# Sums over two taps in f32 for two quarters instead of one, in the middle chunks of an attention and GLU kernel

## The chip, the cores and the metric

The kernel runs on one core of a Trainium2 chip. A core has five engines with queues of their own: TensorE (PE; matrix products, which write to PSUM), VectorE (DVE; elementwise work), ScalarE (ACT; activation functions and copies out of PSUM), GpSimd (POOL) and SyncE (SP), which here issues all DMAs. The engines wait for each other by semaphores. The metric is the device time of one execution in microseconds; less is better.

## The reference

```python
x = A_x                                  # 1 x 2048 x 512
xn = layernorm(x)
q, k, v = split(xn @ wqkv)               # 32 heads of 16
# token s sees s, s-2, ..., s-14: 8 taps, dilation 2
logits = einsum("bhsd,bhswd->bhsw", q, k[s - 2 w]) * 16 ** -0.5
attn = softmax(where(s - 2 w >= 0, logits, -1e9))
o = einsum("bhsw,bhswd->bhsd", attn, v[s - 2 w])
s_ = o @ wo
g = silu((gelu(xn @ w_gate) * (xn @ w_up)) @ w_down)   # 1792 wide inside
return x + s_ * g
```

Matrices are bf16.

## The kernel before

The 2048 tokens go through in four chunks `j` of 512 (`TQ`). For each chunk TensorE runs three stages: `glu` (14 groups `fc` of 128 inner columns; each 4 matmuls into `g_ps` and 4 into `u_ps`), `qkv` of the next chunk (12 groups of 4 matmuls), and `down` (4 token tiles of 14 matmuls into `y_ps`), after which `finish` multiplies in the attention's result (`s_ps`). The attention is fitted in between.

The schedule is manual: each engine's order is the order of the calls. The table `side` lists, by `at(key, fn, ...)`, what is called ahead of a step; `("glu", j, fc)` means ahead of group `fc` of chunk `j`, and so ahead of that group's `h` product on VectorE.

The steps that matter:

- `glu` (L461): ScalarE makes `ge = gelu(g_ps)` and `u` from PSUM, VectorE multiplies them into `h`. `ge` and `u` have three buffers each (`sm`), and the PSUM pool `mm` has four banks.
- `qk_products` (L320): in the qkv stage of the next chunk VectorE makes the 8 products `pk` of `q` with shifted `k`, each in two halves, 16 instructions. `logits` (L339) sums them over the 16 elements of a head on TensorE (`L_ps`), and ScalarE writes `E = exp(L_ps)`. The taps lie in `E` as 4 `wl` on the partitions (32 heads each) times 2 `wh` along the free dimension.
- `load_v` (L300): four DMAs bring `v` into `v_arr`, one for each `wl`, shifted, so that 128 partitions hold 32 heads by 4 taps.
- `av_product(j, g, wh)` (L401): the product of `E` for one `wh` with 4 of the 16 elements of `v` (a quarter `g`), written as bf16 `pv`. In chunks 2 and 3 it is made in two instructions, `n = 2`.
- `av_pair(j, g, d)` (L414): one element of a quarter, both `wh` at once in f32 (`two`), then an addition of the two halves into bf16 `pv`. It does on VectorE the sum over `wh` that otherwise TensorE does.
- `av_sums` (L434): TensorE sums `pv` over the four `wl` for each quarter. A quarter made by `av_product` takes 8 matmuls (4 for each `wh`), one made by `av_pair` takes 4. Each writes 32 partitions, 128x512 moving.
- `sums` (L532), called after the first `y_ps` tile of a chunk (for the last chunk, ahead of glu group 12): denominators, `av_sums`, the next chunk's logits, then the reciprocals, and the loads of the next `v_arr`.

Before the change quarter 0 of chunks 1 to 3 is made by pairs, ahead of groups 2, 4, 6 and 8; the other three quarters by six `av_product`, ahead of 1, 3, 5, 7, 9 and 10. Chunk 0 uses `av_product` alone. The tile `two` shares a buffer with `q_sb` (tag `q` of the pool `qp`, one buffer). `pk` and `pv` rotate through the 12 buffers of the pool `prod`; from chunk 1 on the second four `pk` share a buffer with `v_arr`.

Of the kernel before, what the change touches and what calls it, by code (L numbers as in the profile page):

```python
# [8 lines left out]
ALU = mybir.AluOpType  # L9
AF = mybir.ActivationFunctionType  # L10
BF16 = mybir.dt.bfloat16
F32 = mybir.dt.float32

P = 128
# [5 lines left out]
WH = 2  # L20
PAD = 16
TQ = 512
# [6 lines left out]
def kernel(  # L29
# [13 lines left out]
    nc = tc.nc  # L43
    B, S, D = A_x.shape
    DF = B_w_gate.shape[1]
    NT, NC, NF, NJ = S // P, D // P, DF // P, S // TQ
# [6 lines left out]
    def pool(name, bufs, **kw):  # L53
        return ctx.enter_context(tc.tile_pool(name=name, bufs=bufs, **kw))
# [4 lines left out]
    qp = pool("qp", 1)  # L59
# [3 lines left out]
    prod = pool("prod", 12)  # L63
    hp = pool("hp", 14)
    xtp = pool("xtp", 2)
    op = pool("op", 1)
# [48 lines left out]
    def load_late_weights():  # L115
# [18 lines left out]
        out=vT.rearrange("(k p) n -> p k n", p=P)[:, :, 0:PAD],  # L134
# [134 lines left out]
    st = [dict(pk={}, pv={}, vst={}) for _ in range(NJ)]  # L269

    def copy_out(j, fo, ps, i0=0, n=TQ, m=1, copy=None):

        which, c = divmod(fo, NC)
        if which == 0:
            if "q" not in st[j]:
                st[j]["q"] = qp.tile([P, NC, TQ], BF16, name="q_sb", tag="q")
            dst = st[j]["q"][:, c : c + m, i0 : i0 + n]
        elif which == 1:
            dst = k_sb[j][:, c : c + m, PAD + i0 : PAD + i0 + n]
        else:  # L280
            if c // 2 not in st[j]["vst"]:
                st[j]["vst"][c // 2] = vsp.tile([P, 2, TQ], BF16, name="vst")
            dst = st[j]["vst"][c // 2][:, c % 2 : c % 2 + m, i0 : i0 + n]
        if copy is None:
            nc.scalar.activation(out=dst, in_=ps, func=AF.Copy)  # L285
        else:
            copy(out=dst, in_=ps)
        if which == 2 and (c + m) % 2 == 0 and i0 + n == TQ:
            r, lo = slice((c // 2) * 2 * P, (c // 2 + 1) * 2 * P), PAD + j * TQ
            nc.sync.dma_start(  # L290
                out=vT[r, lo : lo + TQ].rearrange("(c p) n -> p c n", p=P),
                in_=st[j]["vst"][c // 2][:],
            )

    def qkv(j, fo):
        ps = mm.tile([P, 1, TQ], F32, name="qkv_ps", tag="mm")
        project(ps[:, 0, :], wqkv_sb, fo * P, j)
        copy_out(j, fo, ps[:])
# [102 lines left out]
    def av_product(j, g, wh):  # L401
        pv = prod.tile([P, 4, TQ], BF16, name="pv", tag="prod")
        lo = WL * DIL * (1 - wh)
        n = 4 if j < 2 else 2
        for d in range(0, 4, n):
            nc.vector.tensor_tensor(  # L406
                out=pv[:, d : d + n, :],
                in0=st[j]["E"][:, wh, :].unsqueeze(1).to_broadcast([P, n, TQ]),
                in1=st[j]["va"][:, 4 * g + d : 4 * g + d + n, lo : lo + TQ],
                op=ALU.mult,  # L410
            )
        st[j]["pv"][g, wh] = pv

    def av_pair(j, g, d):  # L414

        if d == 0:
            st[j]["pv"][g] = prod.tile([P, 4, TQ], BF16, name="pv", tag="prod")

            st[j]["two"] = qp.tile([P, WH, TQ], F32, name="two", tag="q")
        two = st[j]["two"]  # L420
        v = st[j]["va"][:, 4 * g + d, 0:TQ]
        nc.vector.tensor_tensor(  # L422
            out=two[:],
            in0=st[j]["Eb"][:],
            in1=bass.AP(
                tensor=v.tensor, offset=v.offset, ap=[v.ap[0], [WL * DIL, WH], [1, TQ]]
            ),
            op=ALU.mult,
        )
        nc.vector.tensor_tensor(  # L430
            out=st[j]["pv"][g][:, d, :], in0=two[:, 0, :], in1=two[:, 1, :], op=ALU.add
        )
# [78 lines left out]
    def at(key, fn, *args):  # L511
        side.setdefault(key, []).append((fn, args))
# [16 lines left out]
    for i in range(8):  # L529
        at(("glu", 0, 9 + i) if i < 5 else ("qkv", 1, 0), av_product, 0, i // 2, i % 2)  # L530
# [15 lines left out]
    for j in range(1, NJ):  # L546
        at(("qkv", j, 2), k_halo, j)
        for i in range(2):
            at(("qkv", j, 4 + 4 * i), qk_products, j, range(W), 2 * i, 2)

        for i in range(6):
            at(("glu", j, 1 + i + min(i, 4)), av_product, j, 1 + i // 2, i % 2)
        for d in range(4):
            at(("glu", j, 2 + 2 * d), av_pair, j, 0, d)
    at(("glu", NJ - 1, 12), sums, NJ - 1)


# [4 lines left out]
    pairs = [(8 + 2 * i, mm.tile([P, 2, HQ], F32, name="v_ps", tag="mm")[:]) for i in range(2)]  # L562
# [58 lines left out]
    for fo, ps in pairs:  # L621
        copy_out(0, fo, ps, 0, HQ, 2, nc.vector.tensor_copy if fo >= 8 else None)
# [5 lines left out]
    for n, fo in enumerate((0, 2, 4, 6, 8, 10)):  # L628
        ps = mm.tile([P, 2, HQ], F32, name="qkv_ps", tag="mm")

        w = HQ if n else P
        for i0 in range(0, HQ, w):
            for i in range(2):
                project(ps[:, i, i0 : i0 + w], wqkv_sb, (fo + i) * P, 0, HQ + i0, w)
        copy_out(0, fo, ps[:], HQ, HQ, 2)
# [65 lines left out]
```

## Time and profile before

| what | value |
|---|---|
| median of 5 runs | 226.8 us (226.61 to 226.99) |
| the profiled execution | 226.97 us, of which the span is 225.3 |
| granted TensorE clock | 0.999 |
| VectorE busy | 164.3 us (73%) |
| ScalarE busy | 131.4 us (58%) |
| glu stage of chunk 1 on TensorE | 73.26 to 97.44 us |
| qkv of chunk 2 on TensorE | 97.44 to 107.80 us |
| `sums` of chunk 1 on TensorE (`den_ps`, `o_ps`, `L_ps`) | 110.82 to 114.28 us |
| glu stage of chunk 2 | 126.91 to 151.08 us |
| glu stage of chunk 3, with its sums | 180.55 to 206.56 us |
| `v_arr` loads, issue to landing | 5.3 / 8.5 / 12.6 us (least, median, most) |

Times in the views count from the first instruction of the span. A row of the groups names the line, the engine, the operation, what is written and read, partitions x elements with their types, and the count; then the busy time in us and the mean of one in ns; then the idle time of the engine just ahead of such instructions and what ended most of it. A line of the timeline gives start and length in us, and in brackets the idle time ahead of it and what released it. The page's rows L261 `g_ps` and `u_ps` (57.5 us each), L479 `y_ps` (49.9 us) and L261 `qkv_ps` (37.0 us) hold most of TensorE's time; L332 `pk` (38.9 us), L406 `pv` (32.3 us), L471 `h` (23.5 us) and L422 `two` (14.6 us) most of VectorE's.

### The profile page before, as it was taken

What the parts mean: (1) busy time and instruction counts of PE and PEld (TensorE: products, weight loads), DVE (VectorE), ACT (ScalarE), POOL (GpSimd) and SP (SyncE); (2) the same over time, 40 slices, a digit from 0 to 9 for tenths busy, and PEclk for the clock granted to TensorE, in tenths of its full rate; (3) what the DMA queues carried; (4) which work ended last, traced back from release to release, by engine and by line L of the source; (5) the groups of instructions that cost most, each with busy time, mean ns of one, the idle gap of its engine ahead of it and who ended that gap; (6) DMA issues with size and microseconds to landing.
All of it is one profiled execution on the core that took longest, in us unless ns stands there. A gap on an engine that the chain in (4) does not pass through costs nothing.

```text
span 225.3 us, 3583 instructions
## 1 busy us (share of the span) xinstructions
PE 221.3 (98%) x1322; PEld 106.6 (47%) x1322; DVE 164.3 (73%) x295; ACT 131.4 (58%) x207; POOL 21.6 (10%) x67
## 2 busy tenths in 40 slices
PE   8999999999999999999999999999999999999994
PEld 4994444444444444444444444444444444444443
DVE  5588973999984799819983799944944389992452
ACT  4476679767631767676751476767763357666211
POOL 1025981000120000000040000000000000000000
PEclk9999999999999999999999999999999999999999
DMA  6999699972079910000229950000117950001002
GB/s 196 379 401 264 135 197 150 361 218 96 11 153 200 209 23 0 0 3 1 93 52 214 187 146 3 0 0 0 67 41 156 198 138 1 0 0 30 3 23 70
DMA packets 30258, 24.89 MB, mean 111 GB/s; under 512 B 11040, under 2 KB 29728, under 8 KB 30240
## 3 DMA queue, kind: packets, MB, share of 16 engines
q1 hardware_dynamic: 30240, 24.66, 46.8%
q8 instruction: 10, 0.16, 0.3%
q14 instruction: 8, 0.07, 0.1%
HBM read 18.74 MB, written 4.34 MB: 102 GB/s over the span
## 4 chain that ended last, share of the span: by engine, by line
PE 98%; DVE 0%; ACT 0%; issue 0%
PE y_ps L479 22%; PE g_ps L261 22%; PE u_ps L261 21%; PE qkv_ps L261 16%; PE s_ps L495 6%; PE L_ps L352 3%; PE o_ps L442 3%; PE qk_ps L574 2%; PE v_ps L574 1%; PE warm_ps L244 1%; PE qk_ps L565 1%; PE den_ps L372 0%; PE v_ps L565 0%; PE trb L220 0%; PE tr L220 0%; DVE m L503 0%
## 5 line engine op out<-in xcount | busy, mean ns | idle before, releaser
L261 PE MATMUL g_ps<-xnT,wg_sb 128*128 128x512 bf16 x224 | 57.5, 379 | 0.0
L261 PE MATMUL u_ps<-xnT,wu_sb 128*128 128x512 bf16 x224 | 57.5, 379 | 0.0
L479 PE MATMUL y_ps<-wd_sb,h 128*128 128x512 bf16 (+2 forms) x238 | 49.9, 367 | 0.0
L467 ACT ACTIVATE ge<-g_ps 128x512 bf16<-128x512 f32 x56 | 33.5, 598 | 16.9 <-PE g_ps L261 16.8
L332 DVE TENSOR_TENSOR pk<-q_sb,k_sb 128x1024 bf16<-128x1024 bf16 (+1 forms) x56 | 38.9, 759 | 5.9 <-ACT k_sb L285 5.9
L469 ACT ACTIVATE u<-u_ps 128x512 bf16<-128x512 f32 x56 | 33.5, 598 | 16.6 <-PE u_ps L261 16.6
L261 PE MATMUL qkv_ps<-xnT,wqkv_sb 128*128 128x512 bf16 (+2 forms) x200 | 37.0, 345 | 0.0
L479 PEld LDWEIGHTS <-h 128*128 128x128 bf16 x238 | 22.6, 98 | 26.5 <-issue 1.3
L406 DVE TENSOR_TENSOR pv<-E,v_arr 128x1024 bf16<-128x1024 bf16 (+1 forms) x38 | 32.3, 880 | 3.7 <-DMA v_arr<-vT 3.7
L261 PEld LDWEIGHTS <-wu_sb 128*128 128x128 bf16 x224 | 21.9, 98 | 26.4
L261 PEld LDWEIGHTS <-wg_sb 128*128 128x128 bf16 x224 | 21.7, 98 | 26.6 <-issue 0.8
L471 DVE TENSOR_TENSOR h<-ge,u 128x512 bf16<-128x512 bf16 x56 | 23.5, 420 | 14.2 <-ACT u L469 13.9
L487 ACT ACTIVATE sl<-y_ps 128x512 bf16<-128x512 f32 (+2 forms) x17 | 9.7, 572 | 32.7 <-PE y_ps L479 32.7
L261 PEld LDWEIGHTS <-wqkv_sb 128*128 128x128 bf16 x200 | 18.9, 98 | 17.4
L503 DVE TENSOR_TENSOR m<-s_ps,sl 128x512 bf16<-128x512 f32 (+2 forms) x17 | 11.1, 654 | 19.8 <-PE s_ps L495 19.7
L204 POOL TENSOR_TENSOR rstd<-rstd,mhalf 128x1 f32<-128x1 f32 x12 | 7.0, 583 | 90.7 <-DVE rstd L201 90.7
L495 PE MATMUL s_ps<-wo_sb,oT 128*128 128x512 bf16 (+2 forms) x68 | 14.8, 366 | 0.0
L422 DVE TENSOR_TENSOR two<-E,v_arr 128x1024 f32<-128x1024 bf16 x12 | 14.6, 1216 | 0.0
L454 DVE TENSOR_TENSOR oT<-o_ps,rb 128x1024 bf16<-128x1024 f32 x8 | 9.4, 1218 | 6.8 <-DMA rb<-rs_d 6.5
L285 ACT ACTIVATE vst<-qkv_ps 128x512 bf16<-128x512 f32 x14 | 8.4, 598 | 3.7 <-PE qkv_ps L261 3.7
L285 ACT ACTIVATE k_sb<-qkv_ps 128x512 bf16<-128x512 f32 x14 | 8.4, 602 | 3.2 <-PE qkv_ps L261 3.2
L285 ACT ACTIVATE q_sb<-qkv_ps 128x512 bf16<-128x512 f32 x14 | 8.3, 603 | 3.0 <-PE qkv_ps L261 3.0
(65 smaller groups left out, 143.4 us busy)
## 6 DMA issues: line engine op xcount, KB each, us to landing
v_arr<-vT SPq DMA_DIRECT2D x16, 520.0 KB, 8.5
vT<-vst SPq DMA_DIRECT2D x8, 256.0 KB, 2.2
out_dram<-o_t SPq DMA_DIRECT2D x15, 128.0 KB, 2.9
wg_sb<-in_B_w_gate_dram SPq DMA_DIRECT2D x2, 896.0 KB, 10.0
wu_sb<-in_B_w_up_dram SPq DMA_DIRECT2D x2, 896.0 KB, 12.2
wd_sb<-in_B_w_down_dram SPq DMA_DIRECT2D x1, 1792.0 KB, 11.4
wqkv_sb<-in_A_wqkv_dram SPq DMA_DIRECT2D x4, 384.0 KB, 4.5
x_sb<-in_A_x_dram SPq DMA_DIRECT2D x3, 512.0 KB, 7.8
```

What stands on the lines that cost most here:

```text
L261: nc.tensor.matmul(ps, lhsT=w[:, dk, lo : lo + P], rhs=xnT[j][:, dk, i0 : i0 + n], start=(dk == 0), stop=(dk == NC - 1),)
L285: nc.scalar.activation(out=dst, in_=ps, func=AF.Copy)
L332: nc.vector.tensor_tensor(out=st[j]["pk"][w][:, c0 : c0 + n, :], in0=st[j]["q"][:, c0 : c0 + n, :], in1=k_sb[j][:, c0 : c0 + n, off : off ...
L406: nc.vector.tensor_tensor(out=pv[:, d : d + n, :], in0=st[j]["E"][:, wh, :].unsqueeze(1).to_broadcast([P, n, TQ]), in1=st[j]["va"][:, 4 * ...
L422: nc.vector.tensor_tensor(out=two[:], in0=st[j]["Eb"][:], in1=bass.AP(tensor=v.tensor, offset=v.offset, ap=[v.ap[0], [WL * DIL, WH], [1, T ...
L467: nc.scalar.activation(out=ge[:], in_=g_ps[:], func=AF.Gelu_apprx_tanh)
L469: nc.scalar.activation(out=u[:], in_=u_ps[:], func=AF.Copy)
L471: nc.vector.tensor_tensor(out=h[:], in0=ge[:], in1=u[:], op=ALU.mult)
L479: nc.tensor.matmul(y[:], lhsT=st[j][fc][:, tt * P : (tt + 1) * P], rhs=wd_sb[:, fc, cols], start=(fc == 0), stop=(fc == NF - 1),)
L487: nc.scalar.activation(out=sl[:], in_=y[:], func=AF.Silu)
L495: nc.tensor.matmul(s[:], lhsT=st[j]["oT"][:, g, tt * P : (tt + 1) * P], rhs=wo_sb[:, g, cols], start=(g == 0), stop=(g == NC - 1),)
L503: nc.vector.tensor_tensor(out=m[:], in0=s[:], in1=sl[:], op=ALU.mult)
```

## The change

In chunks 1 and 2, quarters 0 and 1 are made by pairs and quarters 2 and 3 by `av_product`; chunk 3 keeps one quarter by pairs. The calls are spread over other glu groups: in chunks 1 and 2 pairs ahead of groups 1, 2, 3, 5, 6, 8, 10 and 11 and products ahead of 0, 7, 12 and 13; in chunk 3 products ahead of 0, 1, 3, 5, 7 and 9 and pairs ahead of 2, 4, 6 and 8. `av_product` is one instruction in every chunk. `two` becomes a tile of the pool `prod`, allocated once for each chunk, and `q_sb` has its buffer to itself. `av_sums` is unchanged: it looks up which quarters were made by pairs.

```diff
-                st[j]["q"] = qp.tile([P, NC, TQ], BF16, name="q_sb", tag="q")
+                st[j]["q"] = qp.tile([P, NC, TQ], BF16, name="q_sb")
...
     def av_product(j, g, wh):
         pv = prod.tile([P, 4, TQ], BF16, name="pv", tag="prod")
         lo = WL * DIL * (1 - wh)
-        n = 4 if j < 2 else 2
-        for d in range(0, 4, n):
-            nc.vector.tensor_tensor(
-                out=pv[:, d : d + n, :],
-                in0=st[j]["E"][:, wh, :].unsqueeze(1).to_broadcast([P, n, TQ]),
-                in1=st[j]["va"][:, 4 * g + d : 4 * g + d + n, lo : lo + TQ],
-                op=ALU.mult,
-            )
+        nc.vector.tensor_tensor(
+            out=pv[:],
+            in0=st[j]["E"][:, wh, :].unsqueeze(1).to_broadcast([P, 4, TQ]),
+            in1=st[j]["va"][:, 4 * g : 4 * g + 4, lo : lo + TQ],
+            op=ALU.mult,
+        )
         st[j]["pv"][g, wh] = pv
...
         if d == 0:
             st[j]["pv"][g] = prod.tile([P, 4, TQ], BF16, name="pv", tag="prod")
-
-            st[j]["two"] = qp.tile([P, WH, TQ], F32, name="two", tag="q")
+            if "two" not in st[j]:
+                st[j]["two"] = prod.tile([P, WH, TQ], F32, name="two", tag="prod")
...
-        for i in range(6):
-            at(("glu", j, 1 + i + min(i, 4)), av_product, j, 1 + i // 2, i % 2)
-        for d in range(4):
-            at(("glu", j, 2 + 2 * d), av_pair, j, 0, d)
+        if j + 1 < NJ:
+            npair, whole, pairs = 2, (0, 7, 12, 13), (1, 2, 3, 5, 6, 8, 10, 11)
+        else:
+            npair, whole, pairs = 1, (0, 1, 3, 5, 7, 9), (2, 4, 6, 8)
+        for i, fc in enumerate(pairs):
+            at(("glu", j, fc), av_pair, j, i // 4, i % 4)
+        for i, fc in enumerate(whole):
+            at(("glu", j, fc), av_product, j, npair + i // 2, i % 2)
     at(("glu", NJ - 1, 12), sums, NJ - 1)
```

## The prediction

> **What bounds the kernel now.** I read the engines' row of the page first, then the chain of waits, then VectorE's timeline in the stage the change edits.
>
> ```profile
> PE 221.3 (98%) x1322; PEld 106.6 (47%) x1322; DVE 164.3 (73%) x295; ACT 131.4 (58%) x207; POOL 21.6 (10%) x67
> ...
> PE 98%; DVE 0%; ACT 0%; issue 0%
> ```
>
> TensorE is busy for 221.3 of 225.3 us, and the chain that ended last is TensorE for 98%. In order of time the chain has no gap between its first matmul at 0.84 us and the last `y_ps` group, which ends at 221.94. So the kernel gets faster only by TensorE having less to do, and slower only if TensorE is made to wait. The stage in which the sums over taps are made reads so in the chain in order of time (start, length, what), for chunks 0, 1 and 2:
>
> ```profile
> 57.19 1.73 PE o_ps L442 x32
> ...
> 111.04 1.51 PE o_ps L442 x28
> ...
> 164.69 1.51 PE o_ps L442 x28
> ```
>
> Chunk 0 has no quarter by pairs and issues 32 matmuls; chunks 1 and 2 have one and issue 28. The difference, 0.22 us for four matmuls, is the price of a quarter. It is also 1.51 / 7 = 0.216 us for each set of four: the four write different 32-partition strips and run beside each other. (The groups give 379 ns as the mean of one `o_ps` matmul; that is a latency of overlapped instructions and must not be multiplied by the count.)
>
> **What is removed from TensorE.** A second quarter by pairs in chunks 1 and 2 takes away 4 matmuls each, 8 in all, with their 8 weight loads (97 ns each beside matmuls, never on the chain): 2 x 0.216 = **0.43 us**. Chunk 3 keeps one pair quarter and its 28 matmuls: 0. Chunk 0 keeps its work: 0.
>
> **What is added to VectorE.** The rows (forms kept apart):
>
> ```profile
> L406 DVE TENSOR_TENSOR pv<-E,v_arr 128x2048 bf16<-128x2048 bf16 x14 | 16.9, 1218 | 3.7 <-DMA v_arr<-vT 3.7
> L406 DVE TENSOR_TENSOR pv<-E,v_arr 128x1024 bf16<-128x1024 bf16 x24 | 15.4, 683 | 0.0
> L422 DVE TENSOR_TENSOR two<-E,v_arr 128x1024 f32<-128x1024 bf16 x12 | 14.6, 1216 | 0.0
> ...
> L430 DVE TENSOR_TENSOR pv<-two 128x512 bf16<-128x512 f32 x12 | 8.3, 692 | 0.4
> ```
>
> A plain quarter is 2 x 1.218 = 2.44 us (2.73 us where it is halved, in chunk 2). A quarter by pairs is 4 x (1.216 + 0.692) = 7.63 us, so in busy time chunk 1 gains 5.2 us of VectorE work. Whether it fits is read from starts, not durations:
>
> ```profile
> 76.62 0.42 DVE L471 TENSOR_TENSOR h<-ge,u 128x512 bf16<-128x512 bf16 x1 [1.51 <-ACT u L469]
> 76.96 1.22 DVE L406 TENSOR_TENSOR pv<-E,v_arr 128x2048 bf16<-128x2048 bf16 x1
> 78.10 0.42 DVE L471 TENSOR_TENSOR h<-ge,u 128x512 bf16<-128x512 bf16 x1
> 78.43 1.22 DVE L422 TENSOR_TENSOR two<-E,v_arr 128x1024 f32<-128x1024 bf16 x1
> 79.69 0.69 DVE L430 TENSOR_TENSOR pv<-two 128x512 bf16<-128x512 f32 x1
> 80.30 0.42 DVE L471 TENSOR_TENSOR h<-ge,u 128x512 bf16<-128x512 bf16 x1
> ...
> 98.16 0.42 DVE L471 TENSOR_TENSOR h<-ge,u 128x512 bf16<-128x512 bf16 x1 [1.30 <-ACT u L469]
> 101.56 9.72 DVE L332 TENSOR_TENSOR pk<-q_sb,k_sb 128x1024 bf16<-128x1024 bf16 x16 [2.97 <-ACT k_sb L285]
> ```
>
> Start to start, `h` costs 0.34, a plain product 1.14 and a pair 1.87 us (78.43 to 80.30). After the change chunk 1 needs 14 x 0.335 + 4 x 1.14 + 8 x 1.87 = 24.2 us of VectorE. TensorE's glu stage lasts 14 x 1.727 = 24.2 us: nothing is left over, so the spread over the groups decides.
>
> **Running VectorE forward, chunk 1.** It is free at 75.05. The first plain product now stands in front of the first `h`, and waits for `v_arr`: the last of its four loads was issued at 64.5 and took 11.5 us, so it lands at 76.0, where before that product started at 76.96 without waiting. Behind it in the queue is `h` of group 0, and behind that ScalarE's `ge` of group 3 (three buffers). From 76.0 with the starts above: `h` 0 done 77.5, `h` 3, behind three pairs in a row, 84.1; the empty groups 4 and 9 let it catch up; `h` 8 92.5, `h` 13 100.2. `h` f can start no earlier than 75.71 + 1.727 f (98.16 for 13), so the largest lag is 2.9 us, at `h` 3. ScalarE's `ge` 6 started at 84.52 and needs `h` 3's buffers: 0.4 us are left. Were it late, `g_ps` 8 (87.08 on TensorE) needs its bank, and `ge` takes 0.60: another 1.9 us. So TensorE is **2.3 us** from a stall at `h` 3; the same sum gives 2.5 at `h` 8 and more at `h` 6.
>
> After the stage, the 16 `pk` products of the next chunk start at 101.56, on `k_sb`, after 2.97 us idle; VectorE is now free at 100.2, so they start as before and end at 111.2. TensorE reaches them 0.22 us sooner, at 112.34: cover of 1.1 us even for the first logits matmul. Cost: 0. The reciprocal, statistics and division behind them do not move.
>
> **Chunk 2.** `v_arr` lands at 118.2 + 11.3 = 129.5, so the first product waits some 0.8 us behind the last `o_t`; lag at `h` 3 2.7 us; end 153.5 against `pk` at 155.20. Before, it paid halved products, so only 4.3 us are added. **Chunk 3** loses the halving (12 x 0.683 = 8.2 against 6 x 1.218 = 7.3 us) and places its last product at group 9, so it ends near 199.9 instead of 201.30, ahead of the sums at 201.5. No cost; no gain either, since `o_ps` followed `den_ps` without a gap.
>
> **Buffers and ScalarE.** `two` leaves the buffer it shared with `q_sb`; in the `prod` ring of 12, chunks 1 and 2 use 7 tiles as before and chunk 3 8 instead of 7, each last read a stage earlier: 0. `E` of chunks 2 and 3 now waits for VectorE's last product, done 13 us earlier: 0. One order changes: with a product ahead of `h`, the gelu table load of chunks 2 and 3 waits for `g_ps`, where it was loaded early. Chunk 1 already runs so:
>
> ```profile
> 74.21 1.28 ACT L467 ACT_TABLE_LOAD   x1 [3.76 <-PE g_ps L261]
> ...
> 124.11 1.28 ACT L467 ACT_TABLE_LOAD   x1
> ```
>
> In chunk 1 `ge` 0 was done at 76.10 against its bank's reuse at 76.72, and TensorE did not stop. In chunks 2 and 3 I charge 0 by that row; uncovered it is at most its 1.28 us each. The moved DMA issues: none; SyncE's queue keeps its order.
>
> **A rule that speaks against it.** The Trainium skill, "VectorE: DVE Perf Modes", section "The DRAIN you can't avoid", says the next operation does not start until the pipe is empty, and its rules for authors say to keep the number of operations small; the change puts 8 operations in place of 2 products. By that, each costs its whole duration: 14 x 0.42 + 8 x 1.908 + 4 x 1.218 = 26.0 us, so chunk 1 would end at 102.0, 0.4 us past the start of the `pk`; still inside their 1.1 us. The page also says that an operation that is not held starts earlier. The trace has `h` of 0.42 us followed after 0.34, so I take the row: 24.2 us. By both, TensorE does not wait.
>
> **Sum.** 226.97 (the profiled execution: span 225.3 and 1.67 around it) - 0.43 = 226.54. The median shown is 226.8, 0.17 below that execution, so on it **226.37 us**, 0.19% less. What I take for the least change that a measurement of this kernel can tell is 0.2%, 0.45 us: the forecast lies at that edge.
>
> **Rivals.**
> *A, the forecast*, 226.37; its own range 226.1 to 226.6 by the runs' scatter (226.61 to 226.99, half of it 0.19). Chance 0.80.
> *B, VectorE stalls TensorE (slower).* Place: `h` late in glu of chunks 1 and 2, so `ge`, so a PSUM bank. The stage is filled to 100%, which speaks for it; all twelve pairs in the trace within 0.01 us of 1.87 speak against. It decides once pairs cost 0.42 us more each (six pairs before `h` 8 against 2.5 us). At 0.7 more, six make 4.2, so 1.7 us per chunk: 226.37 + 3.4 = 229.8; a late `v_arr`, past 78.3, does the same. Chance 0.12, nearer 228 in its milder form.
> *C, the gain is hidden.* The sums end 0.22 us sooner per chunk, but TensorE then waits as long, for the logits' `pk` or the late table load: 226.8. Against: 1.1 us of cover. Chance 0.08.
> *More than 0.43* has no place: no other TensorE work is removed and no gap exists.
>
> **How the numbers follow.** A straddles the bound: 0.43 is 0.02 short of 0.45, but more than twice the scatter's half, so a repeated comparison would rather show it; I split A 0.52 faster, 0.28 same. C goes to same, 0.36; B is slower, 0.12. Range: A's with C's and a little of B's mild edge, 226.0 to 226.95.
>
> **What would show it.** Right: `o_ps` of chunks 1 and 2 as 24 matmuls of 1.30 us, all else on TensorE of the same length, no gap; VectorE without idle from about 76 to 100, `pk` still released by `k_sb`; the gelu load of chunks 2 and 3 released by `g_ps`. Wrong: a gap of TensorE ahead of `g_ps` 8 or later in a glu stage, `ge` released by VectorE for more than 1.9 us, or `pk` starting after 102.5.

## The result, and the profile after

The changed kernel takes 226.19 us in the median of 21 runs (225.90 to 226.72), the kernel before 226.80 in 41 runs (226.36 to 227.64). The ratio is 0.9976, with a 95% interval of 0.9970 to 0.9983: 0.54 us less, and between 0.39 and 0.68; the two medians lie 0.61 apart. The forecast was 226.37, or 0.43 less.

The page's row of the engines, and the chain that ended last of the changed kernel in order of time (start, length, what), reduced to the two steps that differ from the first glu group on:

```profile
PE 219.9 (98%) x1314; PEld 105.6 (47%) x1314; DVE 172.8 (77%) x295; ACT 130.7 (58%) x207; POOL 21.6 (10%) x67
```

```profile
110.45 1.29 PE o_ps L440 x24
...
163.88 1.29 PE o_ps L440 x24
```

`o_ps` of chunks 1 and 2 went from 28 matmuls in 1.51 us to 24 in 1.29. From there to the end every other step of the chain has the length it had before, to 0.01 us. The two profiled executions lie further apart than that, 226.97 against 225.93 us. The rest is the start: the first glu group stands at 16.86 us of the chain here and at 17.46 before, though nothing ahead of it was changed. TensorE's timelines, before and then changed, show where this begins, in warm-up matmuls on constants:

```profile
2.92 1.91 PE L565 MATMUL qk_ps<-const-bfloat16-1.0,zero 128*128 128x512 bf16 x4
```

```profile
2.92 1.38 PE L567 MATMUL qk_ps<-const-bfloat16-1.0,zero 128*128 128x512 bf16 x4
```

The changed kernel with one quarter by pairs, the first experiment below, took 1.91 us for them again, so the 0.60 us is scatter between executions and no part of the change. 1.04 - 0.60 leaves 0.44, the two `o_ps` groups. A difference of two single profiles would have more than doubled the gain.

VectorE's timeline in the glu stage of chunk 1, changed kernel (start, length, line, operation, then the idle time ahead of it and what ended it):

```profile
76.10 1.22 DVE L404 TENSOR_TENSOR pv<-E,v_arr 128x2048 bf16<-128x2048 bf16 x1 [1.58 <-DMA v_arr<-vT]
...
83.83 0.75 DVE L469 TENSOR_TENSOR h<-ge,u 128x512 bf16<-128x512 bf16 x2
...
99.89 0.41 DVE L469 TENSOR_TENSOR h<-ge,u 128x512 bf16<-128x512 bf16 x1
100.96 9.72 DVE L332 TENSOR_TENSOR pk<-q_sb,k_sb 128x1024 bf16<-128x1024 bf16 x16 [0.66 <-ACT k_sb L285]
```

The stage is as full as foreseen: no idle time from 76.10 to 100.3, and then still 0.66 us until `k_sb`. Ahead of the first `h`, at 77.24, stands the new wait for `v_arr`. ScalarE's timeline shows how near the edge this comes:

```profile
84.34 0.60 ACT L465 ACTIVATE ge<-g_ps 128x512 bf16<-128x512 f32 x1 [0.62 <-DVE h L469]
...
127.04 1.28 ACT L465 ACT_TABLE_LOAD   x1 [3.76 <-PE g_ps L261]
```

`ge` 6 of chunk 1 waited 0.62 us for `h` 3. It ended at 84.94, and TensorE takes its bank for `g_ps` 8 at about 86.3 (13.82 us, 8 groups of 1.727, after the stage's first `g_ps` at 72.5): 1.4 us were left, and TensorE had no gap. The second line is the gelu table load of chunk 2, late as foreseen.

### The profile page after: what moved, and what is told of

It reads as the page before. It is cut to its first block, busy times and chain, and to the rows that moved or that the text cites. A ratio compares the mean times of both kernels' runs of the same rounds, so it can differ in the third digit from the quotient of the medians.

```text
span 224.2 us, 3569 instructions
## 1 busy us (share of the span) xinstructions
PE 219.9 (98%) x1314; PEld 105.6 (47%) x1314; DVE 172.8 (77%) x295; ACT 130.7 (58%) x207; POOL 21.6 (10%) x67
## 4 chain that ended last, share of the span: by engine, by line
PE 96%; DVE 1%; DMA 1%; ACT 0%; issue 0%
PE y_ps L477 22%; PE g_ps L261 22%; PE u_ps L261 22%; PE qkv_ps L261 16%; PE s_ps L493 6%; PE L_ps L352 3%; PE o_ps L440 3%; PE qk_ps L576 2%; DMA x_sb<-in_A_x_dram 1%; PE v_ps L576 1%; DVE stats L187 1%; PE den_ps L372 0%; PE trb L220 0%; PE tr L220 0%; DVE mv L190 0%; DVE m L501 0%
## 5 line engine op out<-in xcount | busy, mean ns | idle before, releaser
L404 DVE TENSOR_TENSOR pv<-E,v_arr 128x2048 bf16<-128x2048 bf16 x22 | 26.6, 1218 | 8.3 <-DMA v_arr<-vT 8.3
L469 DVE TENSOR_TENSOR h<-ge,u 128x512 bf16<-128x512 bf16 x56 | 23.0, 418 | 5.4 <-ACT u L467 5.4
L420 DVE TENSOR_TENSOR two<-E,v_arr 128x1024 f32<-128x1024 bf16 x20 | 24.3, 1217 | 0.0
L428 DVE TENSOR_TENSOR pv<-two 128x512 bf16<-128x512 f32 x20 | 13.8, 692 | 0.7
```

What stands on the lines that cost most here:

```text
L404: nc.vector.tensor_tensor(out=pv[:], in0=st[j]["E"][:, wh, :].unsqueeze(1).to_broadcast([P, 4, TQ]), in1=st[j]["va"][:, 4 * g : 4 * g + 4, ...
L420: nc.vector.tensor_tensor(out=two[:], in0=st[j]["Eb"][:], in1=bass.AP(tensor=v.tensor, offset=v.offset, ap=[v.ap[0], [WL * DIL, WH], [1, T ...
L428: nc.vector.tensor_tensor(out=st[j]["pv"][g][:, d, :], in0=two[:, 0, :], in1=two[:, 1, :], op=ALU.add)
L469: nc.vector.tensor_tensor(out=h[:], in0=ge[:], in1=u[:], op=ALU.mult)
```

## The experiments

**Is the gain in the 8 matmuls?** Two runs take the change apart. The first keeps the whole products and the buffer, gives up the second quarter by pairs, and calls the steps of chunks 1 and 2 where the change calls those of chunk 3:

```diff
-            npair, whole, pairs = 2, (0, 7, 12, 13), (1, 2, 3, 5, 6, 8, 10, 11)
+            npair, whole, pairs = 1, (0, 1, 3, 5, 7, 9), (2, 4, 6, 8)
```

> The changed kernel with one quarter by pairs in chunks 1 and 2 as before; the whole products, the buffer of its own for two, and the new places in the glu groups stay. Theory (the gain is the 8 matmuls taken from TensorE): o_ps is back at 28 matmuls of 1.51 us in chunks 1 and 2, the gain is gone, 226.8 us, ratio to before 1.000. Rival (the gain, or part of it, comes from the other parts of the change): 226.2 us, ratio 0.998, with o_ps at 1.51 us.

Measured: 226.62 against 226.61 us, ratio 0.9999 (0.9991 to 1.0008). The chain in order of time:

```profile
111.17 1.51 PE o_ps L440 x28
```

The whole products, the buffer and these places give nothing by themselves that this comparison, good to 0.2 us each way, can tell. The second run is the kernel before with the second quarter alone:

```diff
...
+        if j + 1 < NJ:
+            for i, fc in enumerate((1, 2, 3, 5, 6, 8, 10, 11)):
+                at(("glu", j, fc), av_pair, j, i // 4, i % 4)
+            for i, fc in enumerate((4, 7, 12, 13)):
+                at(("glu", j, fc), av_product, j, 2 + i // 2, i % 2)
+        else:
...
```

> The kernel before with nothing but the second quarter by pairs in chunks 1 and 2: two still shares the buffer of q_sb, chunk 2 still pays its two products in two instructions each, and no product stands ahead of the first h. Theory (8 matmuls): 226.3 us, ratio 0.998, as the changed kernel; the gelu table load of chunk 2 is early again, and v_arr is not waited for ahead of h. Rival (the buffer or the places are needed, or give part of the gain): a ratio of 1.000 or more.

Measured: 226.24 us, ratio 0.9984 (0.9977 to 0.9990), with the same short `o_ps`:

```profile
110.87 1.29 PE o_ps L442 x24
```

So 0.36 us (0.23 to 0.52), within its interval the 0.43 of two sets of four matmuls; no cost of the shared buffer or of the halved products shows. One thing expected here was wrong: the gelu table load of chunk 2 stood behind `g_ps` all the same (127.46 us, released by it), and in the run ahead of it, which does have a product ahead of the first `h`, it was early (124.23). What the late loads of all runs here share is a product ahead of group 12 or 13 of the chunk before. The likely reason, read from the order of the calls and not tested, is that `E` of the next chunk then waits for VectorE itself, and that the table load carries a different wait for it. It costs TensorE nothing: no gap stands there.

**How far is TensorE from a stall?** A third quarter by pairs in chunks 1 and 2 overfills VectorE:

```diff
-            npair, whole, pairs = 2, (0, 7, 12, 13), (1, 2, 3, 5, 6, 8, 10, 11)
+            npair, whole, pairs = 3, (0, 13), (1, 2, 3, 4, 5, 6, 7, 8, 9, 10, 11, 12)
```

> The changed kernel with three quarters by pairs in chunks 1 and 2: 4 matmuls fewer per chunk again (0.43 us in all), but VectorE needs 12 x 1.87 + 2 x 1.14 + 14 x 0.335 = 29.4 us in a glu stage of 24.2. Theory (TensorE is 2.3 to 2.5 us from a stall): the overrun of 5.2 us goes past the cover, TensorE stalls about 2 us in each of the two chunks, 226.2 - 0.4 + 4 = 230 us, ratio 1.015, with idle time of TensorE in the glu stages of chunks 1 and 2 alone. Rival (VectorE's load does not reach TensorE): 225.8 us, ratio 0.996.

Measured: 232.45 us, ratio 1.0267 (1.0248 to 1.0285). TensorE's timeline in chunk 1 has three gaps from the last glu group on, the first of which is shown, and a fourth of 0.18 us where the last logits wait for `pk`:

```profile
95.68 1.02 PE L261 MATMUL g_ps<-xnT,wg_sb 128*128 128x512 bf16 x4 [0.31 <-ACT ge L465]
```

From the first `g_ps` to the end of the logits chunk 1 took 42.85 us (72.55 to 115.40) against 40.90 in the changed kernel (72.51 to 113.41), with one set of 0.22 fewer: a stall of 2.2 us, as expected. Chunk 2 took 45.20 (127.93 to 173.13) against 40.90, a stall of 4.5, which was not. Both stalls make up the time: 226.19 - 0.43 + 2.2 + 4.5 = 232.5. The chain in order of time, from the store of the reciprocals to the first product of chunk 2, says why the second is larger:

```profile
115.72 2.30 DMA rs_d<-rs
...
122.21 11.21 DMA v_arr<-vT
133.54 1.22 DVE pv L404
```

The reciprocals are queued on VectorE behind the `pk`; their store and reload stand ahead of the next `v_arr` loads on SyncE. A late VectorE stage thus makes the next one begin late: its first product came at 133.54, 4.3 us later than the changed kernel's (129.25), with TensorE only 2.0 later (127.93 against 125.93). The difference, 2.3 us, is the difference of the two stalls: the chain closes on itself, and chunk 2 pays for its own overrun and for the lateness handed on.

Two runs measure the cover directly, by making the f32 product ahead of `h` 3 more than once in chunks 1 and 2:

```diff
-        nc.vector.tensor_tensor(
-            out=two[:],
...
+        for _ in range(2 if (j + 1 < NJ and g == 0 and d == 2) else 1):
+            nc.vector.tensor_tensor(
+                out=two[:],
...
```

The second run has a 4 in place of the 2.

> The changed kernel with the f32 product of the third pair of chunks 1 and 2 (ahead of h 3) made twice: 1.25 us more of VectorE at the place with the least cover, in each of the two chunks; nothing else. Theory (from the changed kernel's profile: ge 6 started at 84.34 in chunk 1, and g_ps 8 takes its bank at 86.5, so 1.5 us are left, 1.8 in chunk 2): no stall, 226.2 us against the changed kernel's 226.2, ratio to before 0.998, with ge 6 about 1.2 us later. Rival (VectorE is already at the edge, every microsecond added reaches TensorE): 226.2 + 2.5 = 228.7 us, ratio 1.008.

> As the run with one product more, with three more: 3.75 us ahead of h 3 in chunks 1 and 2. Theory: 3.75 - 1.5 = 2.2 us of stall at g_ps 8 of chunk 1; the reciprocals, queued on VectorE behind pk, are then some 0.8 us later against TensorE, and with them the next v_arr, so chunk 2 has 1.0 us of cover left and stalls 2.7: 226.2 + 5 = 231 us, ratio 1.020. If the late v_arr did not count: 226.2 + 2.2 + 2.0 = 230.4. Rival (the cover is much larger, as three ge buffers and four banks might give): 227 us or less.

With one product more: 226.81 us, ratio 1.0012 (0.9998 to 1.0025), but the 22 runs spread from 226.08 to 228.36: the fastest are at the 226.2 that was expected, the median is 0.6 above. With three more: 233.87 us, ratio 1.0297 (1.0261 to 1.0332), 2.9 above the expectation. In the second, TensorE's timeline has two gaps in the glu stages, both ahead of `g_ps` 8:

```profile
88.76 1.02 PE L261 MATMUL g_ps<-xnT,wg_sb 128*128 128x512 bf16 x4 [1.82 <-ACT ge L466]
```

```profile
146.22 1.02 PE L261 MATMUL g_ps<-xnT,wg_sb 128*128 128x512 bf16 x4 [3.87 <-ACT ge L466]
```

The gap counts from the modelled end of the group before. By starts, `u_ps` 7 began at 85.91 and takes 0.864, so `g_ps` 8 was due at 86.78 and came 1.98 us late, 0.16 more than the gap. In chunk 1, then, 3.75 us more gave a stall of 1.98, and 1.8 us were covered. In chunk 2 `v_arr` came late and the stall was 3.87 + 0.16 = 4.03, where 2.7 were expected. That is 6.0 us of some 7.7. The rest is the clock: the table of stages (length, then the busy time and count of PE, PEld, DVE, ACT and POOL, then the granted clock, DMA share, GB/s) right after the second gap reads

```profile
146.00:148.00 2.00, 1.78 (x8) 0.77 (x8) 1.97 (x4) 1.64 (x4) 0.00 (x0) 0.87 0.04 8
148.00:150.00 2.00, 2.00 (x6) 0.72 (x5) 1.97 (x4) 1.18 (x2) 0.00 (x0) 0.50 0.00 0
150.00:152.00 2.00, 2.00 (x8) 0.79 (x7) 2.00 (x4) 0.98 (x2) 0.00 (x0) 0.78 0.00 0
```

After 3.87 us of idleness TensorE was granted half its clock for a while; 2 x (0.13 + 0.50 + 0.22) = 1.7 us more: by starts, the two groups from `g_ps` 8 (146.22) to `g_ps` 10 (151.35) took 5.13 us instead of 3.45. After the 1.82 us in chunk 1 the granted clock stayed at 1.00. This fits the Trainium skill, "TensorE: Matmul & The Clock Gate", Part 1, by which an idle window of about 3.4 us brings the half clock back. Sum: 226.19 + 6.0 + 1.7 = 233.9.

**Why does one product more give such a spread?** Three more executions of the same kernel, each with its profile:

> One more look at the kernel with one product more, whose times spread from 226.08 to 228.36 us where the changed kernel's spread from 225.90 to 226.72. Theory (the added 1.25 us leaves about 0.3 us of cover, and by how much v_arr lands late against TensorE differs between executions, since TensorE's first stage starts up to 0.6 us earlier or later): an execution of 226.5 or less has no gap of TensorE in glu; a longer one has a gap ahead of g_ps 8 or later in glu of chunk 1 or 2, of about the time above 226.2. Rival (the spread comes from elsewhere): the longer executions have no such gap.

> As the look before: over 226.5 us with a gap of TensorE in glu of chunk 1 or 2 (theory), or without one (rival).

> As the look before: over 226.5 us with a gap of TensorE in glu of chunk 1 or 2 (theory), or without one (rival).

They took 226.15, 228.16 and 226.12 us. The first and third have no gap of TensorE in a glu stage. The second has one, ahead of `g_ps` 8 of chunk 2. VectorE's first product of that chunk waited long for `v_arr` there, and less in the first execution:

```profile
141.97 1.02 PE L261 MATMUL g_ps<-xnT,wg_sb 128*128 128x512 bf16 x4 [1.56 <-ACT ge L466]
```

```profile
131.82 1.23 DVE L404 TENSOR_TENSOR pv<-E,v_arr 128x2048 bf16<-128x2048 bf16 x1 [3.39 <-DMA v_arr<-vT]
```

```profile
129.68 1.22 DVE L404 TENSOR_TENSOR pv<-E,v_arr 128x2048 bf16<-128x2048 bf16 x1 [1.53 <-DMA v_arr<-vT]
```

SyncE's queue, in the second execution and then in the first:

```profile
112.65 0.33 SPq L389 DMA_DIRECT2D rs_d<-rs  x1
116.09 2.05 SPq L395 DMA_DIRECT2D rb<-rs_d  x4
```

```profile
111.96 0.33 SPq L389 DMA_DIRECT2D rs_d<-rs  x1
113.43 2.70 SPq L395 DMA_DIRECT2D rb<-rs_d  x4
```

From the store of the reciprocals to their reload it took 3.4 us instead of 1.5, with `v_arr` queued behind (118.33 instead of 116.32). So the theory holds in its main point: the longer execution loses 1.7 of its 2.0 us in that gap (1.56 + 0.16). But most of the late `v_arr` comes from the small store, not from TensorE's start.

What stood in the store's way can be read from the DMA view of the second execution (queue and kind, then packets, MB and the share of the 16 DMA engines), from 113.40 to 113.75 us and from 114.95 to 115.30:

```profile
q1 hardware_dynamic: 135, 0.03, 40.2%
q8 instruction: 1, 0.02, 22.7%
```

```profile
q1 hardware_dynamic: 9, 0.00, 7.0%
```

The store has 144 packets. With 135 of them moved, a 16 KB packet of instructions starts (at 113.72; 22.7% of 16 x 0.35 us is 1.27 us). No packet starts until it is over, and then come the last nine, a sixteenth of the store. In the first execution all 144 had started by 113.10, just before the same instruction packet (113.15). In all twelve profiles of this document the store of chunk 1 stands close to that packet: in nine it was through before the packet and took 1.46 to 1.47 us to its reload; with three products more (3.30 us, 114.61 to 117.91) the packet fell among its last nine as here; with three quarters (2.31 us) the packet came just ahead. That the nine wait behind the instruction packet is inferred from this order; the view does not name the DMA engine of a packet. The store of chunk 2 took 1.5 to 2.3 us in these profiles; what delays it there was not followed.

What put the store there is VectorE. With one product more it has no idle time left ahead of the `pk` (0.66 us in the changed kernel), so what chunk 1 is late goes on to the reciprocals: the first product of chunk 1 came at 76.66 in the second execution and at 75.97 in the first, the store at 112.65 and 111.96, both 0.69 us later. Only this one long execution has a profile; whether the others of the 22 were long for the same reason is open.

**A version that beats both.** All four quarters by two whole products and one bf16 addition each, in chunks 1 to 3. It rounds each product to bf16 before the addition, which the f32 pairs do not; what that costs in accuracy no run here shows.

```diff
+    def av_add(j, g):
+        a, b = st[j]["pv"].pop((g, 0)), st[j]["pv"].pop((g, 1))
+        nc.vector.tensor_tensor(out=a[:], in0=a[:], in1=b[:], op=ALU.add)
+        st[j]["pv"][g] = a
...
-        for i, fc in enumerate(pairs):
-            at(("glu", j, fc), av_pair, j, i // 4, i % 4)
...
+        for g in range(NC):
+            fc = 3 * g
+            at(("glu", j, fc), av_product, j, g, 0)
+            at(("glu", j, fc + 1), av_product, j, g, 1)
+            at(("glu", j, fc + 2), av_add, j, g)
```

> The changed kernel with all four quarters of chunks 1 to 3 made as two whole bf16 products and one bf16 addition of 128x2048 in place of the f32 pairs: the sum over the two taps is rounded to bf16 from bf16 products. Theory (o_ps at 54 ns a matmul is what counts, VectorE is free under its cover): o_ps has 16 matmuls in chunks 1 to 3 and 32 in chunk 0, 80 in place of the changed kernel's 108, so 7 sets of 0.216 = 1.5 us less: 224.7 us, ratio to before 0.991. VectorE needs 12 x 1.14 + 14 x 0.335 = 18.4 us in a glu stage. Rival (the last sums of chunk 3 come too late for group 12, or the bf16 addition is no faster than the f32 one): TensorE waits ahead of o_ps of chunk 3, 226 us or more.

Measured: 224.48 us, ratio 0.9912 (0.9898 to 0.9926), 2.0 us less than before. The group of the additions in this kernel, forms kept apart, and TensorE's timeline in chunk 1:

```profile
L414 DVE TENSOR_TENSOR pv<-pv 128x2048 bf16<-128x2048 bf16 x12 | 14.6, 1217 | 0.0
```

```profile
110.94 1.04 PE L445 MATMUL o_ps<-pv,hsum 128*32 128x512 bf16 x16
111.80 1.90 PE L352 MATMUL L_ps<-pk,dsum 128*32 128x512 bf16 x32
```

`o_ps` starts 0.86 us ahead of `L_ps`: four sets. A summed quarter costs VectorE 3 x 1.22 = 3.65 us of busy time in place of 7.63 by f32 pairs: each bf16 operation makes 2048 elements per partition in 1.22 us, where the f32 product makes 1024 in 1.22 and the f32 addition 512 in 0.69. Over the kernel VectorE is busy for 163.0 us, less than before the change (164.3), with nine sets of four matmuls fewer on TensorE (80 of `o_ps` in place of 116): 9 x 0.216 = 1.94 us.

The same for one quarter of chunk 0:

```diff
         at(("glu", 0, 9 + i) if i < 5 else ("qkv", 1, 0), av_product, 0, i // 2, i % 2)
+        if i == 1:
+            at(("glu", 0, 9 + i), av_add, 0, 0)
```

> The kernel with bf16 sums in chunks 1 to 3, and quarter 0 of chunk 0 as well: one bf16 addition of 1.14 us more on VectorE, 4 matmuls fewer. Theory: 0.22 us less than that kernel, 224.3 us, ratio to before 0.990; the pk of chunk 1, which follow chunk 0's products without idle time, end at 59.4 instead of 58.2, and the last of the logits' matmuls needs them at about 60. Rival (they come too late: TensorE waits in L_ps of chunk 1): the same as the kernel with bf16 sums, or more, 224.5 to 225.5 us.

Measured: 224.60 us, ratio 0.9911 (0.9896 to 0.9926). In its profile `o_ps` of chunk 0 has 28 matmuls and `L_ps` of chunk 1 no gap, as the theory has it, but the 0.22 us expected is below what these intervals (0.3 us each way) tell apart, so the gain is open.

## Why the prediction was right

- *The bound.* TensorE's chain without a gap was the whole kernel's time. It fell by what was taken from it, and by nothing else; the run without the second quarter shows the other parts at 0.9999. That the gain is hidden (rival C) did not come: the `pk` ended at 110.68, and the chain reaches their logits at 111.75.
- *The price of a set.* 0.216 us by the difference between chunks 0 and 1, found again as 1.51 - 1.29 = 0.22. The measured 0.54 has 0.43 within its interval (0.39 to 0.68), and the second quarter alone gave 0.36. The median came out 0.18 below the forecast, as much as half the scatter of the runs before (0.19); no run shows a further cause.
- *VectorE in the stage.* First product at 76.0 by the landing of `v_arr`: measured 76.10. `h` 3 done 84.1, measured start 83.83 and end 84.25; `h` 13 done 100.2, measured 100.3; the `pk` still released by `k_sb`. Starts, not durations, were the right ones to add: by whole durations the stage would have ended at 102.0. That the times agree this closely is in part luck: they are set by the landing of `v_arr`, which stayed at 76, while TensorE's stage began 0.6 us earlier (72.51 against 73.10).
- *The cover.* 2.3 us was said for `h` 3. It was too large: the changed kernel's own profile had 1.4 left, 0.6 of the difference by TensorE's earlier start, and the run with three more products shows 1.8 in chunk 1. Of the 0.5 us between 2.3 and 1.8, 0.16 is a slip in the sum: TensorE's starts were taken from the chain (73.26 for the first `g_ps`), whose steps stand that much later than the starts of the timeline (73.10), and ScalarE's from the timeline. Another 0.23 is the execution: TensorE's stage began at 72.96 there, and the first product at 76.09 instead of 76.0. The last 0.1 is not accounted for.
- *The rival of a stalled TensorE* was real, and its threshold was about right (1.4 to 1.8 us instead of 2.3), but its price was too small. The forecast reckoned each chunk by itself. The third quarter shows that a late VectorE reaches the next chunk through `pk`, the reciprocals, their store and the next `v_arr`, and the extra products show that an idle TensorE of 3.9 us then also pays with its clock. The term "1.7 us per chunk" in that rival left out both.
- *The table load.* That it would come late in chunks 2 and 3 was right, and its cost of 0 too. The reason given, a product ahead of `h`, was wrong: with one quarter by pairs such a product is there and the load is early; with the second quarter alone it is not and the load is late. The late load goes with the products ahead of groups 12 and 13.
- *Chunk 3, the buffers, the edge.* No cost was seen, as said. The change lay at the edge of the 0.2%; the measurement put it at 0.24%, between 0.17 and 0.30, and so does not say on which side of 0.2% it lies.

## What to carry to other kernels

Where one engine's chain has no gap, only work taken from that engine counts, and its price is read from two places of the same trace that differ by just that work, not from the mean of overlapped instructions. Work moved to an engine is free up to the point where its stage is full; find that point by adding starts, and follow the late engine round the loop, into the next stage's loads, before pricing an overrun. Before filling an engine with a costly form, look for a cheaper one: here two 16-bit products and one 16-bit addition did the work of four f32 pairs, at another rounding, and gave nearly four times the gain.

## What the runs showed of the hardware

- TensorE, idle for 3.87 us, was granted 0.50 of its clock afterwards, but not at once: it worked again from 146.22 us, had 1.00 until 147 and 0.50 from 148 to 150. Idle for 1.82 us in the stage before, it kept the full clock.
- Four 128x512 matmuls that write four different strips of 32 partitions took 0.216 us together (32, 28, 24 and 16 of them in 1.73, 1.51, 1.29 and 0.86 us), as long as one that writes all 128 (four of `g_ps` in 0.864).
- The 32 KB store of chunk 1 took 1.5 us from issue to its reload in the nine profiles in which it was through before a 16 KB packet of instructions, and 3.4 and 3.3 in the two in which that packet started among its own. With the cover nearly used up, TensorE then stood for 1.56 us.
- Two executions of programs with the same first part differed by 0.60 us at the first glu group, of which 0.5 us came about in four warm-up matmuls (1.91 and 1.38 us): more than the effect under study.
